# A list scheduler's clock in a fused attention and two-layer kernel: DMA loads booked to land later, GpSimd chosen more readily, two key tables moved

## Chip, cores and metric

One core of a Trainium2 chip (trn2) runs the kernel. The metric is the device time of one execution in microseconds (us): the median of the runs, with the lowest and highest beside it. The engines are TensorE (PE, with its weight loads PEld), VectorE (DVE), ScalarE (ACT), GpSimd (POOL) and SyncE (SP), which issues all DMAs.

## What is computed

A causal attention with a decay, its output reshaped to 2304 tokens of 512, then two layers of the same shape with different activations (4 batches, 8 heads, 576 positions, head size 64; hidden size 2048):

```python
def _attn_ref(q, k, v, f):
    scores = scale * np.matmul(q, k.transpose(0, 1, 3, 2))
    cum = np.cumsum(np.log(np.clip(f, 0.0001, 1.0)), axis=-1)
    scores = np.where(causal, -1e9, scores + cum[..., :, None] - cum[..., None, :])
    attn = np.exp(scores - max); attn = attn / (attn.sum(-1) + 1e-09)
    return np.matmul(attn, v)

def _moe_ref(x, w_in, w_out):        # layer 1
    h = x @ w_in
    return (h * (1.0 / (1.0 + np.exp(-h)))) @ w_out

def _moe2_ref(x, w_in, w_out):       # layer 2
    h = x @ w_in
    return (h * np.cos(h)) @ w_out
```

## The kernel before, in words

**The work.** The tokens are cut into nine blocks of 256, the hidden size into eight pieces of 256. For each layer, block and piece there is an "in" step (24 matmuls into the PSUM tile h, L1330) and, once ACT and DVE have made the activation g out of h, an "out" step (24 matmuls into y, L1442, in layer 1; 21, L1221, in layer 2). To keep 32-bit accuracy with 16-bit matmuls, x, the weights and most of attention's operands are scaled by a power of two and split into a high and a low 16-bit part: a copy on ACT, DVE or POOL (L334, L336), a subtraction on DVE (L354). The scale comes from a sum of squares: ACT squares with an accumulator (L359), a one-column matmul on PE adds the partitions up into a tile `nrm`, three or four short DVE operations make the power of two. For x and the weights that matmul is L430, for attention's q and k it is L607.

**Attention** comes as 16 jobs of a first kind (rows 0 to 255 of a pair of heads) and 16 of a second kind (rows 256 to 575). A job of the second kind loads q and k into the single buffer `qs` (L574) and v (L583); ACT squares them; the norm matmul L607 and DVE give the scales; ACT or POOL make the high parts (`qk<-qs`), DVE the low ones (L678), and with the last of these `qs` is free for the next job's load. Then come the scores S (L763, L743, L744), the maximum (L773) with decay rows that are loaded (L645, L651) and masked on POOL (L628, L638), the exponential on ACT (L794), high and low parts of the probabilities (`eh`), their transposes by DMA (L842, L845) or PE (L811), and the output matmuls PV (L938, L949). The output is stored (L960, L963) and loaded again as a block of x (L1192). Blocks 0 to 3 need the first kind, 4 to 7 the second, block 8 all.

**The order.** Nothing of it is written out by hand. Every piece of work is a task with an engine (and sometimes alternatives), a duration, a key and its dependencies; `Scheduler.run` (L110 on) plays them against its own clock and writes each engine's queue in the order in which its clock starts them: of the tasks that are ready on a free engine, the one of the lowest key. The queues are then static and in order on the chip. What its clock believes of a DMA is in L266 to L268: the bytes' time behind 0.65 us, then a landing time by the task's name, `LAND` (L63):

```python
dma_free = max(end + 0.65, dma_free) + best.dma / n * (1.9 if now < 3.2 and best.dma > 0.5 else 1.0)
lanes.append(dma_free + LAND.get(best.name, 0.4))
push(dma_free + LAND.get(best.name, 0.4), "fin", best)
```

Up to the planned time `FILL1` (60 us) PE takes a filler matmul (L411, `spin`) whenever it has nothing ready. Behind the planned time `EARLY`, `apt` (L160) gives a task that has alternatives to the engine where it would end first, with `EXTRA` (L61) added for DVE and for POOL.

Keys: attention's go by a position that `ORDER` and the gaps `GAP4` and `GAP8` count up; layer 1's first weights by `CK0`, `CK1`; the sums, scales and splits of layer 1's second matrix by `C16 + C161 * p` (L1025, eight values of p; the halves are used from block `J16` = 2 on); layer 2's weights by `C2K0`, `C2K1`; the layers' steps by numbers far below these, ahead of everything that is not attention on PE.

Of the kernel before, what the change touches and what calls it, by code (L numbers as in the profile page):

```python
# [41 lines left out]
CK2 = 12  # L42
FILL0 = 0.8
FILL1 = 60
GAP4, GAP8 = 6, 12
CK0, CK1 = 10, 1.6
C2K0, C2K1 = 150, 0.5
W2N0, W2N1 = 30, 1.0
J16, C16, C161 = 2, 60.0, 1.0
QA, QB = 768, 1600  # L50
RA, RB = 512, 960
RQ = 384
# [5 lines left out]
LAT = {"PE": 0.2, "ACT": 0.13, "DVE": 0.1, "POOL": 0.2, "SP": 0.1}  # L58
BULK = ("cload", "w2l", "ldx", "ldq")
FREE = ("s2", "lo", "s", "eh")  # L60
EXTRA = {"DVE": 1.2, "POOL": 1.2}  # L61
BESIDE = ("cb2", "cb3", "clo", "gl", "xlo", "qlo", "rec", "ws")
DSLOW, PSLOW = 1.75, 1.55  # L63
LAND = {"cload": 1.2, "w2l": 1.2, "ldq": 1.0, "ldd": 1.2, "ldx": 1.2, "xt": 1.5}
ENG = ("PE", "ACT", "DVE", "POOL", "SP")
NEG = -8.0e9
MK2 = -1500.0
EARLY, LATE = 40, ()
KDEC, KDP = 12.0, -0.5
INV2PI = 0.15915494309189535  # L70
RND = 12582912.0
# [8 lines left out]
class Scheduler:  # L80
# [10 lines left out]
    def add(self, eng, dur, fn, deps=(), key=0.0, acq=(), rel=(), lat=None, dma=0.0, name="", alts=()):  # L91
        t = Task()
        t.eng, t.dur, t.fn, t.key, t.rel, t.lat, t.dma, t.name = eng, dur, fn, key + KO.get(name, 0), rel, lat, dma, name
        t.alts = {e: (d, f) for e, d, f in [(eng, dur, fn), *alts]}
        t.succ, t.left, t.bulk = [], 0, dma > 0.8 and name in BULK and key > MK2
        if lat is None:
            t.lat = LAT[eng]
        t.acq = [a if isinstance(a, tuple) else (a, len(self.tasks)) for a in acq]
        self.needs(t, deps)
        for tag, o in t.acq:  # L100
            if tag not in FREE:
                self.queue.setdefault(tag, []).append((o, len(self.tasks), t))
        self.tasks.append(t)
        return t
# [12 lines left out]
    def run(self):  # L117
# [10 lines left out]
        def push(t, kind, x):  # L128
            nonlocal cnt
            heapq.heappush(events, (t, cnt, kind, x))  # L130
            cnt += 1
# [42 lines left out]
        while events:  # L174
            now = events[0][0]
            while events and events[0][0] <= now + 1e-9:
                _, _, kind, x = heapq.heappop(events)
                if kind == "busy":
                    e, x = x
                    if moved[e] > now + 1e-9:  # L180
                        push(moved[e], kind, (e, x))
                        continue
                    kind = "fin"
                if kind == "ready":
                    for e in x.alts:
                        ready[e].append(x)
                elif kind == "rel":
                    for r in x.rel:
                        free[r] += 1
                elif kind == "fin":  # L190
                    if x.rel:
                        push(now + SLR, "rel", x)
                    for u in x.succ:
                        u.left -= 1
                        if not u.left:
                            push(now + (0.0 if u.eng == x.eng == "PE" else x.lat), "ready", u)
            progress = True
            while progress:
                progress = False
                for e in ENG:  # L200
                    if busy[e] > now + 1e-9:
                        continue
                    best = None
                    full = len(lanes) >= 8 and lanes[-8] > now + 1e-9
                    if full and e == "SP" and wake < lanes[-8]:
                        wake = lanes[-8]
                        push(wake, "free", None)
                    deep = dma_free > now + QD + 1e-9
                    if deep and e == "SP" and wake < dma_free - QD:
                        wake = dma_free - QD  # L210
                        push(wake, "free", None)
                    for t in ready[e]:
                        if ((best is None or t.key < best.key) and not (full and t.dma) and not (deep and t.bulk)
                                and takes(t) and apt(t, e)):
                            best = t
                    if best is None:
                        if e != "PE" or not FILL0 < now < FILL1 or free["y"] < 2:
                            continue
                        best = self.filler
                    else:  # L220
                        for u in best.alts:
                            ready[u].remove(best)
                        best.eng = e
                        best.dur, best.fn = best.alts[e]
                    for tag, _ in best.acq:
                        free[tag] -= 1
                        if tag not in FREE:
                            head[tag] += 1
                    best.fn()
                    done += best is not self.filler  # L230
                    end = now + best.dur
                    if e == "DVE" and best.name in BESIDE and busy["POOL"] > now:
                        both = min(DSLOW * best.dur, PSLOW * (busy["POOL"] - now))
                        end += both * (1 - 1 / DSLOW)
                        later("POOL", both * (1 - 1 / PSLOW))
                    elif e == "POOL" and busy["DVE"] > now and beside:
                        both = min(PSLOW * best.dur, DSLOW * (busy["DVE"] - now))
                        end += both * (1 - 1 / PSLOW)
                        later("DVE", both * (1 - 1 / DSLOW))
                    if e == "DVE":  # L240
                        beside = best.name in BESIDE
                    if e == "PE":
                        w = int(now / HAM)
                        while win < w:
                            warm = work[win] > 0.7 * HAM
                            win += 1
                            if len(work) <= win:
                                work.append(0.0)
                        if not warm:
                            end += best.dur  # L250
                        a = now
                        while a < end - 1e-9:
                            w = int(a / HAM + 1e-9)
                            while len(work) <= w:
                                work.append(0.0)
                            b = min(end, (w + 1) * HAM)
                            work[w] += b - a
                            a = b
                    if best.dma:
                        n = 2 if best.name == "xd2" else 1  # L260
                        for i in range(n):
                            go = now if i == 0 else end
                            if len(lanes) >= 8:
                                go = max(go, lanes[-8])
                            end = go + best.dur / n
                            dma_free = max(end + 0.65, dma_free) + best.dma / n * (1.9 if now < 3.2 and best.dma > 0.5 else 1.0)  # L266
                            lanes.append(dma_free + LAND.get(best.name, 0.4))
                        push(dma_free + LAND.get(best.name, 0.4), "fin", best)  # L268
                    elif e in moved:
                        moved[e] = end  # L270
                        push(end, "busy", (e, best))
                    elif best is not self.filler:
                        push(end, "fin", best)
                    busy[e] = end
                    push(end, "free", None)
                    progress = True
# [40 lines left out]
def decay_attention_silu_cos_kernel(ctx, tc, qa, qb, f, w1i, w1o, w2i, w2o, out):  # L317
# [38 lines left out]
    def squares(src, n, col):  # L356

        def act():
            nc.scalar.activation(junk[:, 0:n], src(), AF.Square, accum_out=col)  # L359

        return dict(eng="ACT", dur=c_act(n) + 0.02, fn=act)
# [194 lines left out]
    def load_tasks(jb, u):  # L556
# [101 lines left out]
        tl = t0  # L658
        if beta:
            part = lambda c: jb.qs[:, 0:RQ] if c == 0 else jb.qs[:, RQ:RB]  # L660
            tn = [add(**squares(lambda c=c: part(c), n, qn[:, jb.n, c:c + 1]), deps=[t0], key=u - 1, name="sqx")
                  for c, n in ((0, RQ), (1, RB - RQ))]
            if jb.x:
                vf = lambda: jb.v.rearrange("p c a d -> p (c a d)")
                tn.append(add(**squares(vf, QB - RB, qn[:, jb.n, 2:3]), deps=[tv], key=u - 1, name="sqx"))
            tn = add("PE", 0.04, norm, tn, key=u - 10001.0, acq=["s"], name="sc")
            tn = add("DVE", 0.65 if jb.x else 0.4, balance, [tn], key=u - 1, rel=["s"], name="sc")
            by = lambda c: qsc[:, c, jb.n:jb.n + 1]
# [849 lines left out]
```

## Time and profile before

| | us |
|---|---|
| median of the runs (3) | 936.21 |
| lowest, highest | 932.65, 937.88 |
| profiled execution | 931.86 |
| its span, first to last instruction | 930.1 |
| PE busy in it | 901.1 |
| DVE, ACT, POOL busy in it | 765.1, 697.6, 125.4 |

The span is what the trace covers; some 1.8 us lie around it. A busy PE counts fillers too, and a matmul's row is longer than the distance to the next one, so PE's idle time is what the views show as gaps, and a gap's cost is a little more than its length. PE's queue is in order: one waiting matmul holds all behind it.

### The profile page before, as it was taken

What the parts mean: (1) busy time and instruction counts of PE and PEld (TensorE: products, weight loads), DVE (VectorE), ACT (ScalarE), POOL (GpSimd) and SP (SyncE); (2) the same over time, 40 slices, a digit from 0 to 9 for tenths busy, and PEclk for the clock granted to TensorE, in tenths of its full rate; (3) what the DMA queues carried; (4) which work ended last, traced back from release to release, by engine and by line L of the source; (5) the groups of instructions that cost most, each with busy time, mean ns of one, the idle gap of its engine ahead of it and who ended that gap; (6) DMA issues with size and microseconds to landing.
All of it is one profiled execution on the core that took longest, in us unless ns stands there. A gap on an engine that the chain in (4) does not pass through costs nothing.

```text
span 930.1 us, 20926 instructions
## 1 busy us (share of the span) xinstructions
PE 901.1 (97%) x7912; PEld 752.8 (81%) x7912; DVE 765.1 (82%) x1882; ACT 697.6 (75%) x1431; POOL 125.4 (13%) x202
## 2 busy tenths in 40 slices
PE   9989999998999999999999999999999999999997
PEld 5657688776776777887888888888888888888886
DVE  6889898777887898999998865888888888788775
ACT  7999898667768887989878746767666676666663
POOL 6752200111102212331010000000000000000000
PEclk9999999999999999999999999999999999999999
DMA  9985524687986886767757697000000100000010
GB/s 318 384 254 138 170 83 145 128 183 163 217 162 195 229 235 189 211 189 187 268 179 239 210 333 244 16 35 24 24 24 24 45 25 24 1 24 1 23 24 23
DMA packets 113701, 130.03 MB, mean 140 GB/s; under 512 B 63872, under 2 KB 76160, under 8 KB 113600
## 3 DMA queue, kind: packets, MB, share of 16 engines
q1 hardware_dynamic: 113600, 128.70, 47.0%
q8 instruction: 62, 1.02, 0.5%
q14 instruction: 39, 0.32, 0.1%
HBM read 90.25 MB, written 24.72 MB: 124 GB/s over the span
## 4 chain that ended last, share of the span: by engine, by line
PE 44%; DVE 6%; ACT 5%; DMA 5%; issue 2%; SPq 1%; POOL 0%; DVEq 0%; ACTq 0%; POOLq 0%
PE h L1330 23%; PE y L1221 18%; PE y L1442 3%; ACT junk L359 1%; DMA raw<-w2i 1%; DMA w2o_d<-w 1%; DMA x<-x_d 1%; DMA qs<-qb 1%; ACT e L794 1%; DVE e L773 1%; DVE g L354 1%; DVE t L1358 1%; DMA raw<-w2o 1%; DVE w L354 1%; DVE w L493 0%
## 5 line engine op out<-in xcount | busy, mean ns | idle before, releaser
L1330 PE MATMUL h<-x,wi 128*128 128x256 f16 x3432 | 406.0, 273 | 0.0
L1330 PEld LDWEIGHTS <-wi 128*128 128x128 f16 x3432 | 331.6, 98 | 54.0 <-issue 14.2
L1442 PE MATMUL y<-g,rw 128*128 128x256 f16 (+1 forms) x1600 | 223.7, 292 | 2.5 <-ACT g L334 2.3
L1221 PE MATMUL y<-wo,g 128*128 128x256 f16 x1512 | 176.5, 273 | 0.0
L1221 PEld LDWEIGHTS <-g 128*128 128x128 f16 x1512 | 147.6, 98 | 17.1
L1442 PEld LDWEIGHTS <-rw 128*128 128x128 f16 x1344 | 129.4, 98 | 25.4 <-issue 10.5
L1406 ACT ACTIVATE g<-t 128x896 f16<-128x896 f32 x72 | 68.0, 944 | 32.9 <-DVE t L1400 31.8
L1409 DVE TENSOR_TENSOR g<-t,g 128x896 f16<-128x896 f32 x72 | 78.4, 1089 | 16.3 <-ACT g L1406 14.7
L794 ACT ACTIVATE e<-e,su 128x128 f32<-128x128 f32 (+4 forms) x144 | 82.6, 576 | 11.8 <-DVE su L773 11.8
L1384 ACT ACTIVATE t<-h,ru 128x512 f32<-128x512 f32 x72 | 49.1, 682 | 49.7 <-PE h L1330 49.3
L1394 DVE SCALAR_TENSOR_TENSOR t<-h,rg,t 128x512 f32<-128x512 f32 x72 | 54.0, 750 | 35.9 <-ACT t L1391 35.9
L1390 ACT ACTIVATE t<-t,ru 128x512 f32<-128x512 f32 x72 | 51.8, 719 | 32.0 <-DVE t L1387 32.0
L1358 DVE SCALAR_TENSOR_TENSOR t<-t,h 128x512 f32<-128x512 f32 x72 | 49.2, 683 | 21.0 <-ACT t L1355 20.7
L1355 ACT ACTIVATE t<-h,rg 128x512 f32<-128x512 f32 x72 | 48.7, 676 | 22.2 <-PE h L1330 21.0
L773 DVE CUSTOM_DVE_ANT_0 e<-st,dk 128x256 f32<-128x256 f32 (+3 forms) x128 | 59.2, 493 | 5.3 <-PE st L763 2.1
L1387 DVE SCALAR_TENSOR_TENSOR t<-t,ru,h 128x512 f32<-128x512 f32 x72 | 53.6, 744 | 9.6 <-ACT t L1384 8.8
L334 ACT ACTIVATE g<-t,rg 128x512 f16<-128x512 f32 (+1 forms) x72 | 51.4, 714 | 12.6 <-PE y L1442 10.4
L1442 PEld LDWEIGHTS y<-g,rw 128*128 128x128 f32 x256 | 47.3, 195 | 12.8 <-issue 3.4
L1391 ACT ACTIVATE t<-t,halfpi 128x512 f32<-128x512 f32 x72 | 52.0, 722 | 2.3
L354 DVE SCALAR_TENSOR_TENSOR g<-t,rg,g 128x512 f16<-128x512 f32 x56 | 43.9, 784 | 9.3 <-ACT g L334 8.9
L835 DVE SCALAR_TENSOR_TENSOR eh<-e,su,eh 128x512 f16<-128x512 f32 (+1 forms) x66 | 40.4, 637 | 4.6 <-ACT eh L334 3.9
L359 ACT ACTIVATE junk<-qs 128x384 bf16<-128x384 f32 (+1 forms) x32 | 19.2, 600 | 25.1 <-DMA qs<-qb 24.7
(160 smaller groups left out, 1251.3 us busy)
## 6 DMA issues: line engine op xcount, KB each, us to landing
rw<-w1i SPq DMA_DIRECT2D x16, 512.0 KB, 5.8
rw<-w1o SPq DMA_DIRECT2D x16, 512.0 KB, 7.2
x<-x_d SPq DMA_DIRECT2D x16, 512.0 KB, 4.1
dk<-decay_d SPq DMA_DIRECT2D x16, 512.0 KB, 5.1
raw<-w2i SPq DMA_DIRECT2D x16, 512.0 KB, 5.0
raw<-w2o SPq DMA_DIRECT2D x16, 512.0 KB, 5.4
qs<-qb SPq DMA_DIRECT2D x16, 480.0 KB, 4.2
w2o_d<-w SPq DMA_DIRECT2D x24, 256.0 KB, 2.6
```

Of the source, the lines that this page charges most:

```text
L354: fn=lambda: nc.vector.scalar_tensor_tensor(out(), a(), scale(), b(), ALU.mult, ALU.subtract))
L773: nc.vector.tensor_tensor_reduce(out, s, d, -0.125, first, ALU.add, ALU.min, cell["sm"][:, o:o + 1])
L794: nc.scalar.activation(x, x, AF.Exp, bias=sm[:, i:i + 1], scale=-1.0, accum_out=sm[:, 4 + i:5 + i])
L1221: nc.tensor.matmul(y[bank][:, 256 * half:256 * half + 256], g[:, gi, ga], w[:, wi, 256 * col:256 * col + 256], start=p == 0 and half == 0 ...
L1330: nc.tensor.matmul(h[:, i], w[:, wi, 128 * k:128 * k + 128], x[:, xi, k], start=(i == 0 and q == 0 and k == 0), stop=(i == 1 and q == 2 an ...
L1358: nc.vector.scalar_tensor_tensor(cell["t"], cell["t"], 1.0, cell["h"], ALU.add, ALU.mult)
L1387: nc.vector.scalar_tensor_tensor(cell["t"], cell["t"], r, cell["h"], ALU.subtract, ALU.subtract)
L1391: nc.scalar.activation(cell["t"], cell["t"], AF.Sin, scale=-2.0 * PI, bias=halfpi)
L1394: nc.vector.scalar_tensor_tensor(cell["t"], cell["h"], r, cell["t"], ALU.mult, ALU.mult)
L1406: nc.scalar.activation(g_t[s][:, 0], cell["w"], AF.Copy)
L1409: nc.vector.tensor_tensor(g_t[s][:, 1], cell["w"], g_t[s][:, 0], ALU.subtract)
L1442: nc.tensor.matmul(y[:, e * TB:(e + 1) * TB], w[:, wi, 128 * ec:128 * ec + 128], g[:, gi, i * TB:(i + 1) * TB], start=(st and e == 0), sto ...
```

## The change

Only the planner's numbers change; no operation of the computation is added or left out. Loads and stores are booked to land later (`LAND`, up from 1.0 to 1.5 to 2.2 to 3.0 us; others 0.9 for 0.4 us; in the first 30 us 1.2 us for all), their bytes take 1.2 times as long behind 60 us, and at most eight outstanding ones are counted with 1.2 us each. The squares of an attention job's q, k and v hand on after 1.0 us. GpSimd's handicap in the choice of an engine falls from 1.2 to 0.8 us, and the free choice begins at 20 us in place of 40. The second four jobs of attention's first kind come two places later, and the keys of layer 1's second matrix go from 60 to 67 to 70 to 84.

```diff
@@ -42,11 +42,11 @@
 CK2 = 12
 FILL0 = 0.8
 FILL1 = 60
-GAP4, GAP8 = 6, 12
+GAP4, GAP8 = 8, 12
 CK0, CK1 = 10, 1.6
 C2K0, C2K1 = 150, 0.5
 W2N0, W2N1 = 30, 1.0
-J16, C16, C161 = 2, 60.0, 1.0
+J16, C16, C161 = 2, 70, 2.0
 QA, QB = 768, 1600
 RA, RB = 512, 960
 RQ = 384
@@ -58,14 +58,14 @@
 LAT = {"PE": 0.2, "ACT": 0.13, "DVE": 0.1, "POOL": 0.2, "SP": 0.1}
 BULK = ("cload", "w2l", "ldx", "ldq")
 FREE = ("s2", "lo", "s", "eh")
-EXTRA = {"DVE": 1.2, "POOL": 1.2}
+EXTRA = {"DVE": 1.2, "POOL": 0.8}
 BESIDE = ("cb2", "cb3", "clo", "gl", "xlo", "qlo", "rec", "ws")
 DSLOW, PSLOW = 1.75, 1.55
-LAND = {"cload": 1.2, "w2l": 1.2, "ldq": 1.0, "ldd": 1.2, "ldx": 1.2, "xt": 1.5}
+LAND = {"cload": 2.2, "w2l": 2.5, "ldq": 3.0, "ldd": 2.5, "ldx": 2.5, "xt": 2.5, "xd": 1.5}
 ENG = ("PE", "ACT", "DVE", "POOL", "SP")
 NEG = -8.0e9
 MK2 = -1500.0
-EARLY, LATE = 40, ()
+EARLY, LATE = 20, ()
 KDEC, KDP = 12.0, -0.5
 INV2PI = 0.15915494309189535
 RND = 12582912.0
@@ -93,8 +93,7 @@
         t.eng, t.dur, t.fn, t.key, t.rel, t.lat, t.dma, t.name = eng, dur, fn, key + KO.get(name, 0), rel, lat, dma, name
         t.alts = {e: (d, f) for e, d, f in [(eng, dur, fn), *alts]}
         t.succ, t.left, t.bulk = [], 0, dma > 0.8 and name in BULK and key > MK2
-        if lat is None:
-            t.lat = LAT[eng]
+        t.lat = LAT[eng] if lat is None else lat
         t.acq = [a if isinstance(a, tuple) else (a, len(self.tasks)) for a in acq]
         self.needs(t, deps)
         for tag, o in t.acq:
@@ -263,9 +262,9 @@
                             if len(lanes) >= 8:
                                 go = max(go, lanes[-8])
                             end = go + best.dur / n
-                            dma_free = max(end + 0.65, dma_free) + best.dma / n * (1.9 if now < 3.2 and best.dma > 0.5 else 1.0)
-                            lanes.append(dma_free + LAND.get(best.name, 0.4))
-                        push(dma_free + LAND.get(best.name, 0.4), "fin", best)
+                            dma_free = max(end + 0.65, dma_free) + best.dma / n * (1.9 if now < 3.2 and best.dma > 0.5 else 1.0 if now < 60 else 1.2)
+                            lanes.append(dma_free + 1.2)
+                        push(dma_free + (LAND.get(best.name, 0.9) if now > 30 else 1.2), "fin", best)
                     elif e in moved:
                         moved[e] = end
                         push(end, "busy", (e, best))
@@ -658,11 +657,11 @@
         tl = t0
         if beta:
             part = lambda c: jb.qs[:, 0:RQ] if c == 0 else jb.qs[:, RQ:RB]
-            tn = [add(**squares(lambda c=c: part(c), n, qn[:, jb.n, c:c + 1]), deps=[t0], key=u - 1, name="sqx")
+            tn = [add(**squares(lambda c=c: part(c), n, qn[:, jb.n, c:c + 1]), deps=[t0], key=u - 1, lat=1.0, name="sqx")
                   for c, n in ((0, RQ), (1, RB - RQ))]
             if jb.x:
                 vf = lambda: jb.v.rearrange("p c a d -> p (c a d)")
-                tn.append(add(**squares(vf, QB - RB, qn[:, jb.n, 2:3]), deps=[tv], key=u - 1, name="sqx"))
+                tn.append(add(**squares(vf, QB - RB, qn[:, jb.n, 2:3]), deps=[tv], key=u - 1, lat=1.0, name="sqx"))
             tn = add("PE", 0.04, norm, tn, key=u - 10001.0, acq=["s"], name="sc")
             tn = add("DVE", 0.65 if jb.x else 0.4, balance, [tn], key=u - 1, rel=["s"], name="sc")
             by = lambda c: qsc[:, c, jb.n:jb.n + 1]
```

Counted over the two orders, PE has the same matmuls and 89 fillers (L411) in place of 73; POOL has 34 operations more, DVE 28 and ACT 6 fewer. The lines of the changed kernel are one lower from L96 on.

The first place is on ACT, around the squares of q and k of the ninth second-kind job (`junk,qn<-qs`), behind the high parts of the job before it (`qk<-qs`). Before:

```order
L334 ACTIVATE qk<-qs,qsc 128x576
L334 ACTIVATE eh<-e,su 128x3x128 x2
L334 ACTIVATE xo<-pv,inv 128x320
L1355 ACTIVATE t<-h,rg_143 128x512
L794 ACTIVATE e,su<-e,su 128x576
L334 ACTIVATE eh<-e,su 128x4x128
L334 ACTIVATE eh<-e,su 128x64
L334 ACTIVATE g<-t,rg_147 128x512
L1355 ACTIVATE t<-h,rg_143 128x512
L359 ACTIVATE junk,qn<-qs 128x384
L359 ACTIVATE junk,qn<-qs 128x576
```

Now, from the row behind the second `qk<-qs`:

```order
L793 ACTIVATE e,su<-e,su 128x384
L333 ACTIVATE xo<-pv,inv 128x320
L358 ACTIVATE junk,qn<-v 128x640
L333 ACTIVATE g<-t,rg_147 128x512
L793 ACTIVATE e,su<-e,su 128x576
L1354 ACTIVATE t<-h,rg_143 128x512
L333 ACTIVATE eh<-e,su 128x3x128
L333 ACTIVATE eh<-e,su 128x4x128
L333 ACTIVATE eh<-e,su 128x64
L333 ACTIVATE g<-t,rg_147 128x512
L358 ACTIVATE junk,qn<-qs 128x384
L358 ACTIVATE junk,qn<-qs 128x576
```

Ahead of the squares now stand the squares of v, one more high part g of a layer step (two for one), one more exponential (two for one) and one tanh less (L1354 in place of two L1355); in the order of PE the matmul L607 that follows them moves back by layer matmuls in the same way.

The second place is on ACT, where block 7 of x (the first to need the last attention job) is squared and split: `x_6574` before, `x_6924` now; `x_6577` and `x_6934` are block 8. `t<-h` opens a step's activation. Before:

```order
L359 ACTIVATE junk,sq<-x_6574 128x512 x2
L359 ACTIVATE junk,sq<-x_6577 128x512 x2
L334 ACTIVATE g<-t,rg_147 128x512
L359 ACTIVATE junk,sq<-w 128x512
L334 ACTIVATE x<-x_6574,scl 128x512 x2
L1355 ACTIVATE t<-h,rg_143 128x512
L334 ACTIVATE raw<-raw 128x512
L483 ACTIVATE raw<-raw 128x512
L334 ACTIVATE raw<-raw 128x512
L334 ACTIVATE g<-t,rg_147 128x512
L483 ACTIVATE raw<-raw 128x512
L1355 ACTIVATE t<-h,rg_143 128x512
```

Now:

```order
L1354 ACTIVATE t<-h,rg_143 128x512
L333 ACTIVATE w_6993<-raw,scl 128x512
L358 ACTIVATE junk,sq<-w 128x512
L358 ACTIVATE junk,sq<-x_6924 128x512 x2
L333 ACTIVATE g<-t,rg_147 128x512
L358 ACTIVATE junk,sq<-x_6934 128x512 x2
L333 ACTIVATE x<-x_6924,scl 128x512 x2
L333 ACTIVATE w_7076<-raw,scl 128x256
L358 ACTIVATE junk,sq<-w 128x512
L333 ACTIVATE x<-x_6934,scl 128x512 x2
L482 ACTIVATE raw<-raw 128x512
L1354 ACTIVATE t<-h,rg_143 128x512
```

Before, five more steps of block 6 open between the split of block 7 and that block's first step; now the last row is block 7's first step. On PE, 52 matmuls of L1330 and 114 of L1442 now stand between the last PV matmul and block 7's first; 168 and 180 did before. Layer 2's weights are prepared later too: of the 48 stores of prepared pieces, 44 stand ahead of layer 2's first matmul, where all 48 did. Of the 16 jobs' q and k, POOL now makes seven high parts in place of three, and eleven more of the probabilities' (`eh`).

## Rows read from the trace of the kernel before

**Rows 1.** The page, part 1: busy time of each engine, share of the span, instructions.

```profile
PE 901.1 (97%) x7912; PEld 752.8 (81%) x7912; DVE 765.1 (82%) x1882; ACT 697.6 (75%) x1431; POOL 125.4 (13%) x202
```

**Rows 2.** Busy time by stretch; behind each sum (x) instructions, then clock, DMA share, GB/s.

```profile
0.00:60.00 60.00, 56.65 (x373) 35.26 (x373) 45.68 (x143) 53.35 (x159) 40.74 (x61) 1.00 0.97 343
60.00:120.00 60.00, 55.48 (x382) 43.14 (x382) 52.09 (x159) 54.61 (x162) 16.81 (x20) 0.97 0.51 153
120.00:186.00 66.00, 66.00 (x478) 52.88 (x479) 57.08 (x181) 54.27 (x127) 7.32 (x14) 1.00 0.47 119
186.00:376.00 190.00, 177.52 (x1669) 140.19 (x1668) 153.25 (x431) 149.51 (x344) 38.91 (x76) 1.00 0.80 200
376.00:440.00 64.00, 63.99 (x604) 51.29 (x602) 59.35 (x163) 57.85 (x131) 15.15 (x24) 1.00 0.70 186
...
580.00:920.00 340.00, 340.00 (x3121) 304.72 (x3120) 279.98 (x529) 226.32 (x323) 0.00 (x0) 1.00 0.07 23
```

**Rows 3.** Waits of PE: engine, tile, line, releaser: us in total, times, longest.

```profile
PE nrm L607 <- ACT junk L359: 11.3, 10, 1.7
PE nrm L430 <- DVE sq L426: 2.8, 4, 1.0
...
PE pv L938 <- DMA pt<-eh: 1.0, 2, 0.8
```

**Rows 4.** Waits of all engines: ACT for the load of q and k.

```profile
ACT junk L359 <- DMA qs<-qb: 24.7, 11, 4.4
```

**Rows 5.** Timeline 278 to 285 us: start, length, engine, line, operation [idle before].

```profile
278.74 0.43 SPq L574 DMA_DIRECT2D qs<-qb  x1
...
282.86 0.52 ACT L359 ACTIVATE junk<-qs 128x384 bf16<-128x384 f32 x1 [3.60 <-DMA qs<-qb]
...
284.33 0.16 PE L607 MATMUL nrm<-qn,ones 128*128 128x3 bf16 x1 [1.39 <-ACT junk L359]
```

**Rows 6.** DMA issues: tile, queue, count, KB each, median us to landing.

```profile
x<-x_d SPq DMA_DIRECT2D x16, 512.0 KB, 4.1
...
qs<-qb SPq DMA_DIRECT2D x16, 480.0 KB, 4.2
```

**Rows 7.** Groups by line: busy us, mean ns | idle before.

```profile
L1330 PE MATMUL h<-x,wi 128*128 128x256 f16 x3432 | 406.0, 273 | 0.0
...
L336 DVE TENSOR_SCALAR rw<-rw,scl 128x512 f16<-128x512 f32 x10 | 4.7, 495 | 0.0
...
L334 ACT ACTIVATE rw<-rw,scl 128x512 f16<-128x512 f32 x6 | 4.2, 710 | 0.0
```

**Rows 8.** Timeline of PE, 12 us: seven filler matmuls in a row.

```profile
12.38 1.67 PE L411 MATMUL spin<-ones 128*128 128x512 bf16 x7
```

**Rows 9.** Busy time 60 to 80 us, with the granted clock.

```profile
60.00:80.00 20.00, 17.61 (x111) 14.01 (x112) 16.77 (x57) 18.10 (x54) 5.21 (x6) 0.91 0.34 109
```

**Rows 10.** Timeline 437 to 456 us: last attention output, its store, load and split.

```profile
437.12 1.56 PE L949 MATMUL pv<-pt,v 128*64 128x320 f32 x14
...
440.30 0.32 SPq L960 DMA_DIRECT2D x_d<-xo  x1
...
444.44 0.81 SPq L1192 DMA_DIRECT2D x<-x_d  x2
...
448.68 0.63 ACT L359 ACTIVATE junk<-x 128x512 bf16<-128x512 f32 x1
...
453.78 1.41 DVE L354 SCALAR_TENSOR_TENSOR x<-x,scl,x 128x512 f16<-128x512 f32 x2
```

**Rows 11.** Timeline of DVE: one line alone, and beside GpSimd.

```profile
39.16 0.68 DVE L493 SCALAR_TENSOR_TENSOR rw<-rw 128x512 int32<-128x512 int32 x1
...
55.65 1.17 DVE L493 SCALAR_TENSOR_TENSOR rw<-rw 128x512 int32<-128x512 int32 x1
```

**Rows 12.** Timeline of GpSimd at 55 us.

```profile
55.58 1.79 POOL L486 TENSOR_SCALAR rw<-rw 128x512 int32<-128x512 uint16 x2
```

**Rows 13.** Waits of GpSimd for the decay rows that it masks.

```profile
POOL dk L628 <- DMA dk<-decay_d: 54.0, 23, 9.9
```

## The prediction

> **What bounds the kernel now.** First the page's busy table: PE is busy 97% of the span, DVE 82%, ACT 75% [rows 1]. PE is the engine to follow, so the next view is the busy time by stretch, read for where PE is not full [rows 2]. From 580 to 920 us it is: 3121 matmuls in 340.00 us, one every 0.109 us, and all that stands there is fixed work. Three earlier stretches have holes: 0 to 60 us 3.4 us (and the fillers, which count as busy), 60 to 120 us 4.5 us, and 186 to 376 us 12.5 us. From 120 to 186 and from 376 to 440 us PE has no hole, although ACT and DVE run at 82 to 93% there. So what a new order can win is some 20 us of holes plus the fillers, and the largest piece is the third.
>
> What makes these holes is in the waits of PE: the small sum matmul of L607, which scales q and k of one of the sixteen second-kind attention jobs, waits ten times for ACT's sums of squares (L359), 11.3 us together and 1.7 us at most [rows 3]. ACT itself waits eleven times there for the load of q and k, 24.7 us [rows 4]. One instance in order of time: the load is issued at 278.74 us, ACT sits idle 3.60 us until it starts on it at 282.86 us, and PE, whose queue is in order, stands 1.39 us until 284.33 us with all of the layer's matmuls behind that one [rows 5]. The rest is small: four waits of 2.8 us for the same sum in the splits of x and of the weights (L430), and two of 1.0 us for attention's transposes [rows 3].
>
> The cause stands in the planner. For the load of q and k it booked 0.5 us of issue, 0.65, 1.2 for the bytes and 1.0 (LAND): 3.35 us. The median from issue to landing is 4.2 us, as in the instance above, 278.74 to 282.86 [rows 5, 6]. Being 0.85 us short or worse, the planner put the sum matmul ahead of matmuls that could have run.
>
> **The change part by part.** All engines keep their work: the matmuls are the same, and only fillers are added. What moves is the order and, for 34 operations, the engine.
>
> *Norm waits, the ten.* The new booking is 0.5 + 0.65 + 1.45 + 3.0 = 5.6 us, 2.25 us later, and the squares now hand on after 1.0 us in place of 0.13: the sum matmul is put 3.1 us later than before, relative to its load. The longest of the ten waits is 1.7 us, the mean 1.1 [rows 3]. So all should go, unless squares are held on ACT by other work. What fills the time are layer 1's own matmuls, which are always there until 440 us; they are taken from later, not added. A wait that goes also gives back the restart: a matmul lasts 0.273 us but the next starts after 0.109 [rows 2, 7], so 0.16 us for each, 1.6 us for ten. Full price 12.9 us. I take **-11.5**; bounds -4 and -12.9.
>
> *Sums of L430 and the transposes.* The load of x was booked at 3.64 us against a median of 4.1 [rows 6], now at 5.2; attention's transposes by 1.2 us more. Four waits of 2.8 us and 0.6 of restarts, two of 1.0 us [rows 3]: 4.4 us. The weights of layer 2 are now prepared up to the start of layer 2, so new ones of the kind may come. I take **-3**; bounds 0 and -4.4.
>
> *The front.* PE has 89 fillers in place of 73. Seven take 1.67 us [rows 8], so 16 are at most 3.8 us; they cost that only where no wait stood in their place. Between 60 and 80 us PE now stands idle for 2.4 us and its granted clock is 0.91 on average [rows 9], so some 3.6 us at the lower level of 1.2 GHz, worth 1.8 us: fillers in the right place could give back part of both. On the other side ten scaled copies of weights (eight of layer 1's second matrix) and four other steps of its conversion go to ACT, 14 x 0.71 us = 9.9 us (DVE needed 0.495 us for a copy) [rows 7]. ACT is nearly full in the front (53.35 of 60 and 54.61 of 60 us), but has 11.7 us free from 120 to 186 us [rows 2], and the copies are spread there: keys 70 to 84 in place of 60 to 67. I take **+2**; bounds -5 (waits and clock go) and +10 (ACT is in front throughout).
>
> *Later end of attention.* The last attention job now ends further into layer 1, and the next token block needs its output. In the profile the way is: output matmuls end at 438.68 us, store issued 440.30, loaded from 444.44, first squares 448.68, split done at 455.19 [rows 10]: 16.5 us, unhurried. In the new PE order 52 + 114 matmuls stand between the last output and the first matmul of block 7: 166 x 0.109 = 18.1 us (348, or 38 us, before). The second pair of order rows shows the same on ACT: no step between the split and the block's first tanh. The cover is thin but enough: **+0.5**; bounds 0 and +4, the latter if store and loads land 5 us late.
>
> *Start of layer 2.* When its first matmuls run, 4 of the 48 prepared pieces are not stored yet; three copies and four subtractions of some 0.7 us stand among layer 2's first elementwise steps, 5 us on two engines. The matrices they belong to are needed some 30 us later. **+1**; bounds 0 and +5.
>
> *GpSimd's extra work.* 34 operations of some 0.8 us more, among them q and k of seven jobs in place of three. A row shows what this does to DVE: the line that takes 0.68 us alone takes 1.17 us at 55.65 us, while GpSimd runs L486 [rows 11, 12]. 27 us of GpSimd at that ratio could cost DVE up to 11 us, against 28 operations of about 0.495 us that leave it, 13.9 us [rows 7]. DVE is at 81% in the third stretch [rows 2]. So nearly nothing on the path, but PE may meet new short waits: **+2**; bounds 0 and +6.
> The Trainium skill, GPSIMD Engine Reference, section 8 (Key points), says that GpSimd shares its SBUF interfaces with VectorE and contends with instructions that have two SBUF inputs. By that rule, with DVE the bound, 11 would stand in place of the 2 and the sum would be 0; the row above agrees with the rule, the busy table does not make DVE the bound.
>
> Sum: -11.5 - 3 + 2 + 0.5 + 1 + 2 = **-9 us**. The profiled execution took 931.9 us (span 930.1), so 922.9 by its own clock. The median of the runs is 936.2, 4.3 us above it; the same difference there gives 927.
>
> **The rivals.**
> *The waits move.* PE's holes in the third stretch are filled, but attention's chain (squares, scaling, S, max, exp, transposes) is what paces it, so PE waits at S or at the output matmuls instead. For it: DVE and ACT are at 80% in that stretch and at 90% and more in the next [rows 2]. Against it: there PE waits for nothing else today [rows 3], and has no hole from 376 to 440 us with the engines fuller. Four of the 12.9 us remain won: 934.
> *ACT holds the front.* +10 in place of +2, the rest as above: 935.
> *DVE is slowed by GpSimd* so far that it sets the pace from 376 us on, where it is at 93% [rows 2]: 11 us in place of 2, the sum is 0, 936. Against it, the 13.9 us that leave DVE.
> *Slower: GpSimd's queue.* q and k, and eleven upper halves of attention's probabilities, now stand in GpSimd's in-order queue between the maskings of the decay rows, which wait for their loads 23 times, 54.0 us, up to 9.9 [rows 13]. If a masking stands ahead whose load lands after the sum matmul, its job's S waits, and PE with it. 17 groups moved there; at 1 us each on PE 17 us, 927 + 17 = 944. It decides from where the mean wait of 2.3 us exceeds what the planner leaves between; against it, the loads of these rows are booked later too (2.5 for 1.2).
>
> **How the numbers follow.** Forecast 0.60, its own range 920 to 932; the waits move 0.16; ACT holds the front 0.09; DVE slowed 0.07; GpSimd's queue 0.08. About 0.5% (4.7 us) is what a measurement of this kernel tells from no change, so faster means below 931.5 and slower above 940.9. Faster: nearly all of the forecast, a third of the second, a few hundredths of the others: 0.67. Slower: the last, and the edge of the two before: 0.10. Same: 0.23. The range: below, the forecast with all bounds won, 917; above, 940, which leaves out the slower rival and half a case of contention.
>
> **What would show it.** Right: the waits of L607 for ACT under 2 us in all, and ACT's for the load of q and k under 8; PE's holes from 186 to 376 us under 4 us. Front: PE at the same matmul (the first of block 2) 0 to 4 us later than now. Ends: no wait over 1 us before block 7, and layer 2 in step after its first two steps. Wrong: PE's holes as long as now under other lines (L763, L938, L811), or GpSimd rows between its maskings that PE or DVE wait for; then the clock was right but PE was not the engine to win from.

## The result and the profile after

The changed kernel takes 911.98 us (median of 4 runs, 910.97 to 912.59) against 934.83 us (the three runs above and a fourth, 932.65 to 937.88): the ratio is 0.9752, with a 95% interval of 0.972 to 0.9785. The forecast was 927, with a range of 917 to 940. The sign was right; the size was not: 22.9 us by the medians, where 9 were forecast. The profiled execution fell from 931.86 to 911.74 us, its span from 930.1 to 909.9.

These are all the waits of PE in the changed kernel (engine, tile, line, releaser: us in total, times, longest):

```profile
PE y L1441 <- ACT g L333: 2.7, 1, 2.7
PE spin L410 <- DVE ones L372: 1.1, 1, 1.1
PE nrm L429 <- DVE inv L434: 1.0, 1, 1.0
PE nrm L429 <- DVE sq L425: 0.3, 1, 0.3
```

The ten waits of the norm matmul (L607 before, L606 now) for ACT [rows 3] are gone, not shortened, and so is every wait of ACT for the load of q and k [rows 4]. The four of the split's sum (2.8 us) are down to one of 0.3, and those for the transposes no longer appear. The longest wait that is left is for ACT, 2.7 us in the front. The same stretches as in [rows 2], busy time by engine (PE, PEld, DVE, ACT, POOL, clock, DMA share, GB/s):

```profile
0.00:60.00 60.00, 58.94 (x380) 37.03 (x381) 47.47 (x143) 52.87 (x155) 39.70 (x55) 1.00 0.91 330
60.00:80.00 20.00, 16.33 (x115) 12.42 (x114) 18.92 (x57) 19.84 (x59) 4.34 (x6) 0.91 0.54 174
60.00:120.00 60.00, 56.33 (x412) 43.66 (x411) 54.96 (x176) 59.78 (x179) 15.93 (x21) 0.97 0.60 178
...
186.00:376.00 190.00, 190.00 (x1795) 154.35 (x1794) 159.19 (x433) 148.56 (x332) 55.55 (x90) 1.00 0.80 197
376.00:440.00 64.00, 64.00 (x606) 52.37 (x605) 58.30 (x159) 54.95 (x123) 19.86 (x29) 1.00 0.77 180
```

From 186 to 376 us PE has no hole, where it had 12.5 us of them, and gets 1795 matmuls started in place of 1669. What is left stands at 66 to 70 us, with a mean granted clock of 0.91 from 60 to 80 us, as before. Summed over the whole span, PE's idle time between the first and the last matmul fell from 22.1 to 4.1 us.

The ninth second-kind job, the instance of [rows 5], in the timeline of the changed kernel (start, length, engine, line, operation):

```profile
266.43 0.38 SPq L573 DMA_DIRECT2D qs<-qb  x1
...
270.69 0.72 ACT L333 ACTIVATE g<-t,rg 128x512 f16<-128x512 f32 x1 [0.58 <-PE y L1441]
271.31 0.51 ACT L358 ACTIVATE junk<-qs 128x384 bf16<-128x384 f32 x1
...
275.76 0.17 PE L606 MATMUL nrm<-qn,ones 128*128 128x3 bf16 x1
```

The load takes as long as ever: its median to landing is 4.2 us as in [rows 6]. No engine stands waiting for it: ACT does a high part g and then the squares, back to back, and the sum matmul starts 9.3 us after the load's issue where it came after 5.6.

### The profile page after: what moved, and what is told of

It reads as the page before. It is cut to its first block, busy times and chain, and to the rows that moved or that the text cites. A ratio compares the mean times of both kernels' runs of the same rounds, so it can differ in the third digit from the quotient of the medians.

```text
span 909.9 us, 20973 instructions
## 1 busy us (share of the span) xinstructions
PE 899.1 (99%) x7928; PEld 753.0 (83%) x7928; DVE 760.6 (84%) x1854; ACT 694.9 (76%) x1425; POOL 160.7 (18%) x236
## 4 chain that ended last, share of the span: by engine, by line
PE 93%; ACT 3%; DVE 2%; DMA 1%; issue 1%; DVEq 0%; ACTq 0%; SPq 0%
PE h L1329 40%; PE y L1441 20%; PE y L1220 18%; PE pv L948 2%; PE spin L410 2%; PE st L762 2%; PE tt L810 2%; PE pv L937 2%; PE st L755 1%; ACT junk L358 1%; PE st L743 1%; PE st L768 1%; DMA rw<-w1i 1%; PE st L742 1%; PE h L1318 0%
## 5 line engine op out<-in xcount | busy, mean ns | idle before, releaser
L1408 DVE TENSOR_TENSOR g<-t,g 128x896 f16<-128x896 f32 x72 | 78.4, 1089 | 14.9 <-ACT g L1405 13.1
L1354 ACT ACTIVATE t<-h,rg 128x512 f32<-128x512 f32 x72 | 48.9, 680 | 29.3 <-PE h L1329 28.9
L333 ACT ACTIVATE e<-e,su 128x256 f32<-128x256 f32 (+4 forms) x78 | 35.2, 509 | 0.9 <-DVE inv L434 0.5
```

Of the source, the lines that this page charges most:

```text
L333: nc.scalar.activation(dst, src, AF.Copy, scale=scale)
L1408: nc.vector.tensor_tensor(g_t[s][:, 1], cell["w"], g_t[s][:, 0], ALU.subtract)
```

## Where the time came from

Each of PE's matmuls is counted at the median distance to the next start of its kind, and fillers at nothing. The sum is the work that PE has done by any time, and two traces can be compared at equal work. It is good to about 1 us while attention runs:

```
work done (us)      60     100    130    180    260    360    460    520    600
before, at (us)     83.7   126.4  156.1  206.3  292.3  388.9  485.2  547.7  628.9
after, at (us)      84.8   123.5  153.6  202.9  279.9  372.5  467.8  528.0  608.7
difference         +1.1   -2.8   -2.5   -3.4  -12.4  -16.4  -17.3  -19.7  -20.2
```

So the front (work up to 130) gives 2.5 us, attention beside layer 1 (work 130 to 460) 14.9 us, and the end of layer 1 with the start of layer 2 gives 2.8 us; from then on the two run at the same pace.

## Experiments: which part of the change does it

Three theories stood against each other. **A**: the clock wins; a plan that books loads as they land is one that PE can keep. **B**: the front and GpSimd win about half. **C**: any new order moves the time by several us. The first four kernels are made from the kernel before.

**The clock alone** (`e1_clock`):

```diff
-LAND = {"cload": 1.2, "w2l": 1.2, "ldq": 1.0, "ldd": 1.2, "ldx": 1.2, "xt": 1.5}
+LAND = {"cload": 2.2, "w2l": 2.5, "ldq": 3.0, "ldd": 2.5, "ldx": 2.5, "xt": 2.5, "xd": 1.5}
...
-... name="sqx")
+... lat=1.0, name="sqx")
```

and the lines of the change on `dma_free` and `lanes`.

> The kernel before with the new clock alone: the later landings, the 1.2 for the bytes, the count of outstanding loads and the 1.0 us behind the squares; GpSimd's handicap, the early choice, the two places and the eight keys stay as before. Theory A (the clock wins: a plan that books loads as they land is a plan that PE can keep): the waits of the norm matmul L607 for ACT fall from 11.3 us to under 2, PE's holes from 186 to 376 us from 12.5 to under 3, and 13 to 18 us of the 23 are there: 917 to 922. Theory B (the front and GpSimd win about half): 924 to 929. Theory C (any new order moves the time by several us either way, this one by luck): the waits need not go, any time from 910 to 935.

Measured: 917.36 us (916.71 to 917.97), ratio 0.9833 (0.9819 to 0.9848): 15.8 us. Waits of PE:

```profile
PE tt L810 <- ACT e L333: 4.5, 1, 4.5
PE nrm L429 <- DVE sq L425: 2.2, 4, 1.0
```

PE is busy for 189.83 of the 190 us from 186 to 376. Time and waits are as A said; the time alone also lies in C's range, but C gives no reason for the waits to go. The front gains nothing here (the wait of 4.5 us stands at 69 us): at work 130 this run is some 1.5 us behind the kernel before, where the changed kernel is 2.5 us ahead.

**All but the clock** (`e2_rest`):

```diff
-GAP4, GAP8 = 6, 12
+GAP4, GAP8 = 8, 12
-J16, C16, C161 = 2, 60.0, 1.0
+J16, C16, C161 = 2, 70, 2.0
-EXTRA = {"DVE": 1.2, "POOL": 1.2}
+EXTRA = {"DVE": 1.2, "POOL": 0.8}
-EARLY, LATE = 40, ()
+EARLY, LATE = 20, ()
```

> The kernel before with all but the clock: GpSimd's handicap 0.8, free choice from 20 us, the four jobs two places later, the keys 70 to 84. Theory A: the waits for loads stay (L607 for ACT 9 to 13 us, ACT for the load of q and k 20 to 28 us), 932 to 940. Theory B: the front gives 5 to 10 us, 925 to 930. Theory C: anything from 925 to 945.

Measured: 942.24 us (940.87 to 945.04), ratio 1.0103 (1.0086 to 1.012), **9 us slower**. That is beyond A (932 to 940) and B (925 to 930), and inside C (925 to 945), so C was still open. The norm waits are as long as before, in fewer pieces:

```profile
PE nrm L607 <- ACT junk L359: 11.2, 6, 3.5
PE nrm L430 <- DVE sq L426: 5.0, 7, 1.4
```

ACT's wait for the load of q and k fell to 13.5 us, where A had 20 to 28. So the parts don't add up: the four numbers cost 9.0 us under the old clock and give 5.4 (917.36 to 911.98) under the new one, or 7.0 when each of the two kernels is set against the kernel before in its own session.

**One booking alone**, the load's (`e3_ldq`) and the squares' (`e4_lat`):

```diff
-LAND = {... "ldq": 1.0, ...}
+LAND = {... "ldq": 3.0, ...}
```

> The kernel before with one number changed: the load of q, k and v is booked to land 3.0 us behind its bytes in place of 1.0. My prediction's step (ten waits, full price 12.9 us) says that L607 waits under 2 us for ACT, and 922 to 926. If the wait only moves along the chain, PE's holes from 186 to 376 us stay at 8 us or more under other lines, and 931 to 936.

```diff
-... name="sqx")
+... lat=1.0, name="sqx")
```

> The kernel before with one number changed: the squares of q, k and v hand on 1.0 us after their end in place of 0.13. The norm matmul comes 0.87 us later relative to its load. Of ten waits of 1.1 us in the mean, some 0.8 us each go: L607 for ACT 3 to 4 us in place of 11.3, ACT's wait for the load as before (20 to 28 us), 926 to 930. Theory C: anything from 925 to 945 with waits unlike these.

Measured: 929.71 us (ratio 0.9965, 0.9945 to 0.9985) and 932.32 us (0.9987, 0.9973 to 1.0001). Each takes its own wait away (L607 for ACT 0.3 us in the first, 0.5 in the second, from 11.3) and neither gives back what that was worth. The waits of PE and its busy time from 186 to 376 us (177.52 before), in the first, then in the second:

```profile
PE nrm L430 <- DVE sq L426: 7.3, 9, 1.5
...
PE pv L938 <- DMA pt<-eh: 2.3, 4, 1.2
...
186.00:376.00 190.00, 185.02 (x1729) 148.16 (x1728) 156.64 (x434) 153.47 (x346) 36.88 (x71) 1.00 0.83 205
```

```profile
PE nrm L429 <- DVE sq L425: 12.3, 13, 3.1
...
186.00:376.00 190.00, 185.78 (x1740) 146.18 (x1738) 158.21 (x446) 153.57 (x351) 40.25 (x79) 1.00 0.84 203
```

So the stretch itself did gain: its holes fell from 12.5 to 5.0 and 4.2 us, and neither run has the 8 us or more under other lines that a wait moving along attention's chain would leave. The time was lost elsewhere in the new order. In the first, the front is some 5 us behind the kernel before at work 130, with 96 fillers in place of 73. In the second, some 5 us go between work 400 and 460, most of it at one wait of L429, 3.1 us long, that ends at 482.6 us and has 3.4 us at the lower granted clock (1.2 GHz) behind it. The other loads are still booked too short, and the sum of the splits (four waits of 2.8 us before) now falls into nine and thirteen waits. Both expectations missed, since they priced the one wait and let the rest of the order stand. That a booking which is still too short causes each of these losses isn't shown. (In the second, ACT's wait for the load also fell, to 11.3 us, which I hadn't expected.)

## Experiments: what the other four numbers are for

Here a quantity of the program itself helps. `Scheduler.run` plays the whole kernel through while it is built; its `now` at the end is the planner's end. The start it gives to every group of layer matmuls can be set beside the chip's start of the same matmuls in the trace, chip minus plan:

```
planned time (us)   86     190    275    379    510    871
before             +3.5    +9.0  +18.5  +24.7  +27.4  +29.5
after              +2.8    +3.4   +4.2   +5.4   +6.0   +6.9
```

Read so, the old plan was never kept: it promised an end at 900.7, where the chip's span was 930.1. The new one promises less (903.9) and is kept to 6 us. With each of the four numbers put back alone in the changed kernel, the planner's end rises, by as much as 17 us, which the expectations used as a price:

```diff
-GAP4, GAP8 = 8, 12
+GAP4, GAP8 = 6, 12
```

> The changed kernel with the second four jobs at their old places (GAP4 6). Theory A, in the form that the runs so far give it (with the new clock the chip needs 6 to 7 us more than the planner's own clock says, 909.9 for 903.9 and 914.9 for 907.6; with the old one 23 to 33 more): the planner's clock ends this order at 921.3, so a span of 927 to 929 and a time of 929 to 931, 17 us slower than the changed kernel, from one number that is worth less than 5.4 us if parts add up. Rival (parts add up, all four together are worth the 5.4 us between 917.4 and 912.0): 912 to 917. Rival (any reordering): 905 to 935 with no tie to the planner's end.

```diff
-J16, C16, C161 = 2, 70, 2.0
+J16, C16, C161 = 2, 60.0, 1.0
```

> The changed kernel with the old keys of layer 1's second matrix (60 to 67). Planner's end 914.3: a span of 920 to 922, 922 to 924. Parts add up: 912 to 917. My prediction's term for the front (the scaled copies on ACT cost 2 us) has it 2 us faster, 910.

```diff
-EARLY, LATE = 20, ()
+EARLY, LATE = 40, ()
```

> The changed kernel with the free choice of engine from 40 us on. Planner's end 920.1: a span of 926 to 928, 928 to 930. Parts add up: 912 to 917.

```diff
-EXTRA = {"DVE": 1.2, "POOL": 0.8}
+EXTRA = {"DVE": 1.2, "POOL": 1.2}
```

> The changed kernel with GpSimd's old handicap (1.2); GpSimd has 28 us less work by the planner's durations, DVE 10 and ACT 10 more. Planner's end 909.9: a span of 916 to 918, 918 to 920. If GpSimd's work slows DVE (my rival with 11 us), taking it away makes DVE's rows shorter and the time 905 to 910. Parts add up: 912 to 917.

Measured: 931.32, 924.16, 930.85 and 918.43 us. All four fall where the planner's end had put them (929 to 931, 922 to 924, 928 to 930, 918 to 920; the first three 0.3, 0.2 and 0.9 us beyond), none where adding up the parts would (912 to 917). Three of the numbers cost 12 to 19 us when they alone are undone, far more than all four undone together (5.4 us). GpSimd's handicap costs 6.5 us, and this can't be told from the cost of all four: its run's ratio to the kernel before (0.9823, 0.9781 to 0.9865) overlaps that of the clock alone.

Most of the loss stands at one place, and it is the one that the prediction had called thin: the first step of block 7, which needs the last attention output. Timeline of the changed kernel, from the last store of that output to the first matmul of block 7:

```profile
450.04 0.42 SPq L962 DMA_DIRECT2D x_d<-xo  x1
...
451.06 1.19 SPq L1191 DMA_DIRECT2D x<-x_d  x2
...
459.29 0.63 ACT L358 ACTIVATE junk<-x 128x512 bf16<-128x512 f32 x1
...
463.39 1.41 DVE L353 SCALAR_TENSOR_TENSOR x<-x,scl,x 128x512 f16<-128x512 f32 x2 [0.45 <-ACT x L333]
...
464.51 1.47 PE L1329 MATMUL h<-x,wi 128*128 128x256 f16 x12
```

This way takes 14.5 us, and PE doesn't wait. In the run with GAP4 6 (`u_gap`) the same store is issued 11.7 us later, and PE has nothing else left. (The planner's position counts on behind a gap, so GAP4 and GAP8 move all of attention that follows, not four jobs alone.)

```profile
461.72 0.50 SPq L962 DMA_DIRECT2D x_d<-xo  x1
...
466.41 0.42 SPq L1191 DMA_DIRECT2D x<-x_d  x1
...
468.36 0.18 PE L429 MATMUL nrm<-sq,ones 128*128 128x1 bf16 x1 [2.75 <-DVE sq L425]
...
473.92 0.18 PE L429 MATMUL nrm<-sq,ones 128*128 128x1 bf16 x1 [5.38 <-DVE sq L425]
...
476.21 1.20 PE L1329 MATMUL h<-x,wi 128*128 128x256 f16 x4 [1.19 <-ACT x L333]
```

Busy time in stretches of 20 us, first of the changed kernel, then two of that run:

```profile
460.00:480.00 20.00, 19.93 (x186) 17.55 (x185) 17.98 (x51) 18.33 (x41) 6.00 (x7) 1.00 0.73 231
...
460.00:480.00 20.00, 7.94 (x63) 5.92 (x61) 16.45 (x41) 16.09 (x34) 4.38 (x5) 0.74 0.89 295
480.00:500.00 20.00, 17.93 (x151) 15.15 (x150) 18.66 (x46) 15.18 (x33) 2.71 (x3) 0.92 0.60 195
```

PE stands idle for 12 of the first 20 us in that run, and the granted clock is at its lower level, 1.2 GHz, from 469.65 to 483.31 us: for 7.1 us behind the first matmul of block 7, some 3.5 us on top of the waits. With GpSimd's old handicap (`u_ext`) the front comes out some 4 us ahead of the changed kernel's at equal work, and 9.6 us are lost at block 7.

The run with the free choice from 40 us on (`u_ear`) loses in the front too: at work 130 it is 4.5 us behind the changed kernel, with one wait of PE at 68 us more than twice as long as there (2.7 us):

```profile
PE y L1441 <- ACT g L333: 5.8, 1, 5.8
```

So under the new clock it is the early choice that makes the front faster, and GpSimd's lower handicap that costs there. `u_ext` also prices GpSimd's extra work behind the front: between 186 and 440 us GpSimd is busy 20.2 us less in it (55.17 for 75.41), and DVE's instructions, compared shape by shape, are some 3 to 4 us shorter in all. DVE does slow beside GpSimd, but no hole of PE comes of it: in the changed kernel PE is busy for all of these 254 us.

Two runs join these findings: GpSimd's old handicap for the front alone (`c1_early`), and with it GAP8 10 (`b1`), which puts attention from the ninth job of the first kind on two places earlier and gave the lowest planner's end.

```diff
-            mine = t.alts[e][0] + EXTRA.get(e, 0.0)
+            extra = {"DVE": 1.2, "POOL": 1.2} if now < 70 else EXTRA
+            mine = t.alts[e][0] + extra.get(e, 0.0)
...
-                    if wait + d + EXTRA.get(u, 0.0) < mine:
+                    if wait + d + extra.get(u, 0.0) < mine:
```

> The changed kernel with GpSimd's old handicap of 1.2 up to the planned time 70 us and 0.8 behind it: the front of the run with the old handicap was 3 to 4 us ahead of the changed kernel, and its loss stood only at block 7. Parts add up: 908 to 910. Theory A with the cliff at block 7: the planner's clock ends at 914.5, so the store of the last attention output comes too late for block 7 again, PE waits 5 us or more there (L429 for DVE) with some 10 us at half clock behind it, and 921 to 924.

```diff
-GAP4, GAP8 = 8, 12
+GAP4, GAP8 = 8, 10
```

> The same with GAP8 10 in place of 12 (the second four jobs' second kind two places earlier). The planner's clock ends at 900.6, the lowest of the orders played through. Theory A: a span of 906.6 to 908.6 and 908 to 911, no wait above 0.5 us at block 7. Any reordering: 905 to 930.

Measured: 925.69 us for the first, 1.7 beyond the forecast and with the wait at block 7 that was expected. Its waits of PE (lines one higher than in the changed kernel):

```profile
PE nrm L430 <- DVE sq L426: 14.5, 7, 9.2
```

The second takes **909.53 us** (909.05 to 909.73), ratio 0.9723 (0.9688 to 0.9758): the last store is issued at 434.81 us, block 7 starts 20.6 us behind it, and the waits of PE of half a microsecond or more are six short ones with the start's among them:

```profile
PE y L1442 <- ACT g L334: 1.8, 1, 1.8
PE h L1330 <- DMA wo<-w2o_d: 1.1, 1, 1.1
PE tt L811 <- ACT e L334: 1.1, 1, 1.1
PE spin L411 <- DVE ones L373: 1.1, 1, 1.1
PE nrm L430 <- DVE sq L426: 1.0, 1, 1.0
PE pv L949 <- ACT junk L359: 0.5, 1, 0.5
```

None of them is at block 7, as the expectation had it. This kernel beats the kernel before. Against the changed kernel its runs don't overlap (910.97 to 912.59), but the two were timed in different sessions, and the intervals of their ratios do; 2.4 us is what the medians say.

## Experiments: how late is late enough

The landings booked 0.7 us earlier (`m_minus`) and 1.5 us later (`m_plus`) than in the changed kernel:

```diff
-LAND = {"cload": 2.2, "w2l": 2.5, "ldq": 3.0, "ldd": 2.5, "ldx": 2.5, "xt": 2.5, "xd": 1.5}
+LAND = {"cload": 1.5, "w2l": 1.8, "ldq": 2.3, "ldd": 1.8, "ldx": 1.8, "xt": 1.8, "xd": 0.8}
```

> The changed kernel with every named load booked 0.7 us earlier. The booked way of q and k is then 4.9 us, over the median of 4.2 but under the longest of 5.65, and the 1.0 us behind the squares stays. The planner's clock ends at 903.6. If the booking need only be above the usual landing: 910 to 913, waits of PE as in the changed kernel. If the margin carries (late landings come through): waits of L606 for ACT and of L429 come back, 2 to 6 us in all, and 914 to 920.

```diff
-LAND = {"cload": 2.2, "w2l": 2.5, "ldq": 3.0, "ldd": 2.5, "ldx": 2.5, "xt": 2.5, "xd": 1.5}
+LAND = {"cload": 3.7, "w2l": 4.0, "ldq": 4.5, "ldd": 4.0, "ldx": 4.0, "xt": 4.0, "xd": 3.0}
```

> The changed kernel with every named load booked another 1.5 us later, beyond what the traces show of them. The planner's clock ends at 948.0. If the planner's end sets the time whatever it believes, 952 to 957. If its order costs nothing where the loads are there early (the chip doesn't wait for what has landed), the chip ends before the planner: 925 to 945, with a chip-minus-plan of zero or below.

Measured: 918.04 and 952.05 us. The first is in the range that the margin had, but not by the place: ACT's wait for the load of q and k came back (6.3 us in three), yet no wait of L606 did, L429 waits 3.6 us in five, and half of the extra lateness against the plan (6.7 us at the planned time 140, where the changed kernel has 3.2) arises in the front. What does that there is open. (Its expectation calls 5.65 us the longest landing; in the kernel before one of the 16 loads of q and k, the first, took 7.5 us.) The second is slower than the kernel before, and its time is at the lower edge of what the planner's end alone had said (952 to 957). Its waits of PE:

```profile
PE nrm L429 <- DVE sq L425: 22.7, 8, 5.9
PE nrm L606 <- ACT junk L358: 2.6, 1, 2.6
```

They lie at 400 to 423 and 489 to 502 us: loads booked so late push attention's jobs back until blocks of x come too late, and the chip, which has the loads earlier, makes up little (chip minus plan falls by 2.9 us at the first place and by 4.2 at the second, which is block 7). A wait that the planner puts into the order is as real as one that it overlooks.

All the runs, planner's end against the chip's span:

```
             plan    span    chip - plan
before       900.7   930.1   29.4    old clock
e4_lat       900.7   931.4   30.7
e3_ldq       905.8   928.4   22.6
e2_rest      906.4   939.1   32.7
e1_clock     907.6   914.9    7.3    new clock
after        903.9   909.9    6.0
u_ext        909.8   918.4    8.6
u_c16        914.3   922.3    8.0
c1_early     914.5   924.5   10.0
u_ear        920.1   929.8    9.7
u_gap        921.3   927.8    6.5
b1           900.6   907.0    6.4
m_minus      903.6   916.9   13.3    0.7 us earlier
m_plus       948.0   950.9    2.9    1.5 us later
```

Under the new clock the order of the planner's ends is nearly the order of the times; across clocks it says nothing: two of the three lowest ends belong to slow kernels. This is what speaks against theory C: eight orders whose planned ends spread over 20.7 us all end 6.0 to 10.0 us behind them.

## Why the prediction was wrong

**The norm waits: right, and a little more.** The forecast for this stretch was -11.7 (the ten waits, the transposes and block 7); measured were -14.9 (work 130 to 460). The holes there before add up to 12.5 us: the ten waits of L607 (11.3), two for the transposes (1.0) and one of 0.2. With thirteen restarts of 0.16 us that makes 14.6: the stretch gave everything. Above the forecast lie the 1.4 us that I had kept back for squares held on ACT (none were), the transposes at their full price, and block 7, which cost nothing.

**The failing step: the costs, the front's above all.** Of the sum -11.5 - 3 + 2 + 0.5 + 1 + 2 the four positive terms, 5.5 us, were to be paid for the new order. The runs showed a gain of 2.5 us in the front in place of its cost, and no cost that could be found for the others:

| term | forecast | measured |
|---|---|---|
| front | +2 | -2.5 |
| norm waits, transposes, block 7 (work 130 to 460) | -11.7 | -14.9 |
| L430, start of layer 2 | -1.3 | -2.8 |
| GpSimd's extra work (behind the front) | +2 | 0 |
| sum | -9 | -20.2 |

(The -3 for L430 and the transposes is split here as their 3.4 and 1.0 us, into -2.3 and -0.7.) The front's +2 had the wrong sign, and it left the early choice of engine without a price: under the new clock that choice is worth some 4.5 us there (`u_ear`), and GpSimd's lower handicap costs some 4 of what the front could gain (`u_ext`). The front's sixteen fillers took the place of waits: PE's holes up to 60 us went from 3.4 to 1.1 us, and the waits at 106 to 111 us are gone. ACT took the extra copies and was busy 59.78 of 60 us from 60 to 120 us, yet PE's waits for it up to 130 us fell from 5.1 to 2.7 us. By the sign that I had named the front came out as forecast (the first matmul of block 2 starts at 174.4 us, at 172.8 before), but that was the wrong yardstick: at equal work PE was ahead, with more of attention behind it.

I had priced each moved piece as a disturbance of an order that stays. But the planner lays the whole order anew around its clock, and a wait that its clock foresees it fills with other work. The run with the clock alone and the one without it show that prices of parts can't be added: -15.8 and +9.0 us would make -6.8, and both changes together gave -22.9.

**The offset: wrong.** To the profiled clock's 922.9 I added the 4.3 us by which the median of three runs stood above the profiled run. After the change the offset is 0.2 us (911.98 to 911.74). In part the 4.3 was chance: with the fourth run it is 3.0, and the later medians of the kernel before (933.21, 934.47, 934.95) stand 1.4 to 3.1 us above the same profile. The runs also scatter less now, over 1.6 us in place of 5.2; the other three kernels with an old booking spread over 4 to 6 us, those with the new clock over 0.7 to 3.6. That the scatter comes from loads landing now earlier, now later is likely but not shown. The offset is 4.1 us of the miss of 15; the sum is 11.2.

**The rivals.** "The waits move" did not happen: no hole is left from 186 to 376 us. A single booking comes near its 934 (929.7 and 932.3 us), but by another way, with losses in the front or behind attention; that the times are near is luck. "ACT holds the front" and the queue of GpSimd did not happen: none of PE's waits in the changed kernel names POOL. "DVE slowed by GpSimd" fell by its size: some 3 to 4 us over 254 us, not 11, and none on PE. The Trainium skill's rule (GPSIMD Engine Reference, section 8, Key points) on GpSimd and VectorE contending has the direction right here and decides nothing.

**Right** was block 7: cover thin but enough. How thin, five runs showed (`u_gap`, `u_ear`, `u_c16`, `u_ext`, `c1_early`); its bound of "+4" was much too low for orders so near, since some 10 to 17 us are lost there once the cover fails.

## What to carry to other kernels

Where a program orders its own work by a clock, set the planned starts beside the trace's before pricing any wait: a gap between them that grows (29 us here) shows that a truer clock can win. Here the clock alone gave 15.8 us and the whole change 22.9, while one booking alone gave 3.5 or 0.9, since the new order lost the rest elsewhere. Tune the other numbers only after the clock, since numbers chosen under a wrong one do not carry over; and book a margin, not more: here 0.7 us less cost 6 us and 1.5 us more cost 40. Look for the one place where two long chains meet (here attention's last output and block 7), because an edit that seems far away is paid there.

## What the runs showed that was not expected

The waits of PE at block 7 cost more than their length: in the six runs that have them (the five above and `m_plus`; 5 to 14 us idle) the granted clock went to 1.2 GHz for 10.2 to 13.7 us, and came back only 6.1 to 7.9 us behind the first matmul of block 7. And the fastest version has no such stretch in the front either: PE's clock is 1.00 from 60 to 120 us in `b1`, where the kernels before and after had 3.41 us at the lower level. `m_plus`, the slowest, has none in the front either; why is not settled.
